# Attention and mixture of experts on one core: exponentials shifted by a running maximum of past batches

## The chip, the cores and the metric

The kernel runs on one core of a Trainium2 chip. A core has TensorE (matrix products, PE in the profile; its weight loads are PEld), VectorE (DVE), ScalarE (ACT), GpSimd (POOL) and SyncE (SP, which here only issues DMAs). The metric is the device time of one execution in microseconds. Before the change it is 1301.42 us, the median of 3 runs (1299.91 to 1301.48).

## The reference, cut to what matters

```python
# q, k, v: 8 batches x 8 heads x 576 rows x 64, standard normal x 0.1
scores = q @ k.T / sqrt(64)                              # 576 x 576 a head
kth  = 32nd largest of each row
scores = where(scores >= kth, scores, -1e9)
scores = scores - max(scores, axis=-1)
attn = exp(scores); attn = attn / (sum(attn) + 1e-9)     # per row
x = attn @ v                                             # heads side by side: 4608 rows x 512
# then top-1 mixture of 8 experts on x: w_gate 512 x 8, w1 512 x 1024, relu, w2 1024 x 512,
# each row scaled by its gate's softmax value
```

Only the 32 largest scores of a row take part. A softmax doesn't change if another number than the row's own maximum is subtracted, as long as the exponentials and their sum are shifted alike.

## The kernel before, in words

**Stages.** First attention over all batches, then the experts. The attention stage has 144 steps of two row tiles (128 rows x 576 scores each); 9 steps are a group `n` of four heads, 18 steps a batch `b`. The stage is a software pipeline: in pass `t` of the loop at line 996 the program issues, in this order, the exponentials of step t-4 (`exps`), the masks of step t-2 (`softmax`), the scores of step t+3 (`scores`, `scores_left`), the products with v of step t-5 (`av`), the transposes of step t-3 (`transp`), and the selection of step t (`topk`). Each engine takes its own instructions in that order; semaphores order the engines.

**One step.** TensorE writes the scores of two row tiles to PSUM; ScalarE copies them to an SBUF tile `sb` (7 pairs of buffers) and SyncE stores them to DRAM as well (for the search below). VectorE runs 24 MAX8 of 48 scores each (line 1016; the 8 largest of each twelfth of a row). `topk` then merges these lists: its list `two` is issued right behind the 24 MAX8, its list `three_` is kept as `delayed` and issued between the MAX8 of the next step, one item behind every second MAX8 (lines 1014 to 1023). In `two` there are two 72-wide MAX8 (`second`), which write places 1 to 8 of the row's work area `v`, and `minus`, which writes places F0 = 8 to 15 from the tile `mid`. `three_` ends in a GpSimd product that makes `nb`: the row's maximum (times -0.125) and its 32nd value (times just under -1). ScalarE's Sign with `nb` as bias marks which scores are under the 32nd value and counts them (`cnt`); GpSimd adds the marks to `sb` (line 471), so that dropped scores become hugely negative.

**The shift.** Line 468 spreads the row's negated maximum to a 128 x 128 bf16 tile `nr` on GpSimd. `transp` first writes these maxima to the transposed scores' PSUM tile `tt` with four bf16 matmuls against an identity (line 484), then adds nine transposes of the scores to them (line 487). `exps` takes the exponential of all of `tt`. The sum of a row is made apart, in `j_sums`, from the 32 values that VectorE found, shifted by the same `nr`.

**Jobs.** What isn't done in every step (loading and turning q and k, sums, writing rows, searching and redoing the rows whose count isn't 32, routing) are generators in lanes. Each says what it needs next (`need(dve=1.0)`, a PSUM bank, a spot), and `advance` lets each lane take at most one part a pass, in order of due time, while the engines' limits (line 52) allow. Parts are put into queues: `dq` for VectorE (issued one at a time between the items of `two`), `aq` for ScalarE, `gq` for GpSimd (at the end of the pass), `pq` for TensorE ahead of the next scores and `lq` for TensorE behind the transposes. `j_find` looks up to 128 rows of a batch whose count is off; it makes `key`, then an index `fl` on VectorE, and gathers the rows; `j_redo` and `j_patch` compute them again; `j_route` assigns experts.

Of the kernel before, what the change touches and what calls it, by code (L numbers as in the profile page):

```python
# [46 lines left out]
TADV = 5  # L47
FREE = (1, 2, 3, 4, 5)
# [3 lines left out]
LIMITS = dict(pool=3.5, act=1.6, dve=2.6, pe=3.0)  # L52
# [3 lines left out]
def attention_moe(ctx, tc, q, k, v, w_gate, w1, w2, out):  # L56
# [130 lines left out]
    nc.vector.memset(factors[:, :, 0], -0.125)  # L187
# [53 lines left out]
    NBB = []  # L241
    for i in range(2):
        NBB.append(jobs.tile([128, NLT, 2], F32, name=f"nb{i}", bufs=1))
# [8 lines left out]
    VQ, CNT, NB, NR = {}, {}, {}, {}  # L252
# [4 lines left out]
    cell, held, att_open = [1], [0], [True]  # L257
# [13 lines left out]
    def need(**k):  # L271
        return k
# [23 lines left out]
    three = psum.tile([128, NB9 * 128], F32, name="tt")  # L296
# [110 lines left out]
    def topk(t, us):  # L407
# [12 lines left out]
        mid = work.tile([128, 2, 8], F32, name="mid", bufs=1)  # L420
# [13 lines left out]
        def second(i):  # L434
# [12 lines left out]
        two.append((minus, (v[:, :, F0:V0, None], mid[:, :, :, None])))  # L447

# [78 lines left out]
    def j_sums(n):  # L527
# [3 lines left out]
        nr = NR[n].rearrange("p (s i) x -> p i s x", i=2)[:, :, :, 0:1]  # L531
# [10 lines left out]
        yield need(pool=0.5)  # L542
# [1010 lines left out]
```

## Time and profile before

| | |
|---|---|
| median of 3 runs | 1301.42 us (1299.91 to 1301.48) |
| profiled execution | 1295.44 us |
| its span, first to last instruction | 1293.4 us |
| busy in the span: PE, DVE, ACT, POOL | 1230.2, 1016.9, 819.1, 859.2 us |
| PE weight loads (PEld) | 972.3 us |
| mean granted TensorE clock | 0.987 |

The table is from one execution under the hardware profiler. Busy time of an engine is the time in which one of its instructions was recorded; an instruction that waits for a semaphore isn't busy. Two neighbouring records of one engine can overlap, since an engine begins an instruction while the one before still runs out. Matmul ends are modelled. A wait is named by the instruction whose semaphore came last.

### The profile page before, as it was taken

What the parts mean: (1) busy time and instruction counts of PE and PEld (TensorE: products, weight loads), DVE (VectorE), ACT (ScalarE), POOL (GpSimd) and SP (SyncE); (2) the same over time, 40 slices, a digit from 0 to 9 for tenths busy, and PEclk for the clock granted to TensorE, in tenths of its full rate; (3) what the DMA queues carried; (4) which work ended last, traced back from release to release, by engine and by line L of the source; (5) the groups of instructions that cost most, each with busy time, mean ns of one, the idle gap of its engine ahead of it and who ended that gap; (6) DMA issues with size and microseconds to landing.
All of it is one profiled execution on the core that took longest, in us unless ns stands there. A gap on an engine that the chain in (4) does not pass through costs nothing.

```text
span 1293.4 us, 33358 instructions
## 1 busy us (share of the span) xinstructions
PE 1230.2 (95%) x10223; PEld 972.3 (75%) x10223; DVE 1016.9 (79%) x6585; ACT 819.1 (63%) x1675; POOL 859.2 (66%) x1172
## 2 busy tenths in 40 slices
PE   5999999999999999998998988999999999999997
PEld 2677776776776776776675766889899999888996
DVE  6999999999999999999999995846683333433763
ACT  3998898898897897897896863332333233233442
POOL 3777876787886886886886886756554333244654
PEclk8999999999999999999999999999999999999999
DMA  6655664664664664664664444645555334346773
GB/s 175 205 169 179 181 205 140 178 192 143 188 181 134 182 183 139 175 189 140 175 190 130 150 126 130 200 124 165 158 163 171 115 106 119 107 156 221 220 210 101
DMA packets 269788, 210.70 MB, mean 163 GB/s; under 512 B 134854, under 2 KB 212834, under 8 KB 269600
## 3 DMA queue, kind: packets, MB, share of 16 engines
q1 hardware_dynamic: 259216, 185.62, 48.3%
q0 software_dynamic: 9152, 22.58, 5.4%
q8 instruction: 82, 1.34, 0.5%
q14 instruction: 106, 0.87, 0.2%
q10 hardware_dynamic: 1232, 0.30, 0.1%
HBM read 102.29 MB, written 107.40 MB: 162 GB/s over the span
## 4 chain that ended last, share of the span: by engine, by line
PE 56%; DVE 21%; POOL 8%; ACT 5%; issue 4%; DMA 4%; SPq 1%; POOLq 0%; ACTq 0%; DVEq 0%
PE ph L1199 16%; PE y L1214 15%; DVE vq L1016 10%; PE px L501 5%; PE pt L260 5%; PE ps L362 5%; POOL sb L471 5%; PE tt L487 4%; DVE vq L1023 4%; PE tt L484 2%; ACT sb L364 1%; DMA sc<-sb 1%; PE mt L1179 1%; PE px L377 1%; ACT sg L470 1%
## 5 line engine op out<-in xcount | busy, mean ns | idle before, releaser
L471 POOL TENSOR_TENSOR sb<-sb,sg 128x576 f32<-128x576 f32 x288 | 369.2, 1291 | 141.4 <-ACT sg L470 82.9
L1016 DVE MAX8 vq<-sb 128x8 f32<-128x48 f32 x3456 | 420.5, 203 | 3.3 <-ACT sb L364 2.6
L949 POOL TENSOR_TENSOR wl<-r,wh 128x512 fp32r<-128x512 f32 x102 | 132.5, 1301 | 206.6 <-DVE wh L948 201.4
L501 PEld LDWEIGHTS px<-et,rv 128*64 128x64 f32 x3200 | 160.2, 139 | 111.7 <-issue 53.2
L470 ACT ACTIVATE sg<-sb,nb 128x576 int8<-128x576 f32 x288 | 223.5, 776 | 25.7 <-POOL nb L1019 19.9
L501 PE MATMUL px<-et,rv 128*64 128x128 f32 (+1 forms) x3200 | 193.8, 270 | 6.3 <-ACT r_et L260 4.4
L1200 ACT ACTIVATE hh<-ph 128x320 fp32r<-128x320 f32 (+2 forms) x128 | 56.1, 438 | 218.8 <-PE ph L1199 196.9
L362 PE MATMUL ps<-qk 64*128 64x512 f32 (+1 forms) x576 | 182.6, 641 | 3.1 <-ACT sb L364 2.6
L492 ACT ACTIVATE et<-tt 128x1152 f32<-128x1152 f32 x144 | 163.1, 1133 | 30.1 <-PE tt L487 29.9
L364 ACT ACTIVATE sb<-ps 128x1024 f32<-128x1024 f32 x144 | 146.8, 1019 | 49.2 <-PE ps L362 49.1
L487 PE MATMUL tt<-turner,sb 128*128 128x128 f32 x1296 | 167.1, 274 | 1.0 <-POOL sb L471 0.9
L1199 PE MATMUL ph<-xh,wh 128*128 128x320 f32 (+2 forms) x504 | 161.0, 319 | 0.0
L1199 PE MATMUL ph<-xh,wl 128*128 128x320 f32 (+2 forms) x504 | 156.5, 310 | 0.0
L1199 PE MATMUL ph<-xl,wh 128*128 128x320 f32 (+2 forms) x504 | 156.3, 310 | 0.0
L1201 DVE SCALAR_TENSOR_TENSOR hl<-ph,hh 128x320 fp32r<-128x320 f32 (+2 forms) x128 | 62.6, 489 | 118.9 <-ACT hh L1200 103.3
L487 PEld LDWEIGHTS tt<-turner,sb 128*128 128x128 f32 x1296 | 139.8, 141 | 1.6 <-POOL sb L471 1.6
L1214 PE MATMUL y<-wh,hl 128*128 128x512 f32 x316 | 124.2, 393 | 2.4 <-DVE hl L1201 2.3
L1214 PE MATMUL y<-wl,hh 128*128 128x512 f32 x316 | 124.3, 393 | 0.0
L1214 PE MATMUL y<-wh,hh 128*128 128x512 f32 x316 | 124.3, 393 | 0.0
L949 DVE TENSOR_TENSOR wl<-r,wh 128x512 fp32r<-128x512 f32 x102 | 85.2, 836 | 49.3 <-ACT wh L946 37.3
L1023 DVE MAX8 vq<-vq 128x8 f32<-128x48 f32 (+1 forms) x576 | 121.6, 212 | 0.0
L1199 PEld LDWEIGHTS ph<-xh,wh 128*128 128x128 f32 x504 | 95.5, 190 | 4.2 <-issue 2.1
(261 smaller groups left out, 2338.2 us busy)
## 6 DMA issues: line engine op xcount, KB each, us to landing
r<-in_moe_w_dram SPq DMA_DIRECT2D x204, 256.0 KB
sc<-sb SPq DMA_DIRECT2D x128, 288.0 KB
sc<-sb SPq DMA_DIRECT2D x128, 256.0 KB
rv<-in_v_dram SPq DMA_DIRECT2D x32, 256.0 KB
xs<-xm SPq DMA_DIRECT2D x16, 512.0 KB
rq<-in_q_dram SPq DMA_DIRECT2D x60, 128.0 KB
rk<-in_k_dram SPq DMA_DIRECT2D x60, 128.0 KB
sc<-sb SPq DMA_DIRECT2D x32, 144.0 KB
```

The source lines that it names most:

```text
L362: nc.tensor.matmul(MAINS[:, n], qk[:, 0, w], qk[:, 1, 2 * LEFT:], start=True, stop=True)
L364: nc.scalar.activation(bass.AP(EX[-1].tensor, EX[-1].offset, [list(EX[-1].ap[0]), [S + LEFT, 2], [1, M]]), MAINS, AF.Copy)
L470: nc.scalar.activation(upper(SG[i]), SB[u], AF.Sign, bias=nb[:, i, 1:2], accum_out=CNT[b][:, 2 * lt + i:2 * lt + i + 1])
L471: nc.gpsimd.tensor_tensor(SB[u], SB[u], SG[i], op=OP.add)
L487: nc.tensor.matmul(tt[:, c], x[:, c * 128:(c + 1) * 128], ident, start=False, stop=c in (3, 7, 8), is_transpose=True)
L492: nc.scalar.activation(ET[t], three.rearrange("p (c q) -> p c q", c=NB9), AF.Exp, scale=0.125)
L501: yield lambda kb=kb, blk=blk: nc.tensor.matmul(px[h * 64:(h + 1) * 64], block(rv, p % 2, kb if kb < MAIN else MAIN + n, h), et[:, blk, q] ...
L949: (nc.gpsimd if i else nc.vector).tensor_tensor(lo, r, hi, op=OP.subtract)
L1016: one[m][0](*one[m][1])
L1023: f(*a)
L1199: nc.tensor.matmul(ph, a[:, c, :], x[:, c, s], start=(m == 0), stop=(m == len(seq) - 1))
L1214: nc.tensor.matmul(PY[u, t], a[:, s], x, start=(f == 0 and m == 0), stop=(f == FC - 1 and m == 2))
```

## The change

- `transp` is nine plain transposes. The four matmuls of line 484 and the tile `nr` are gone.
- `exps` subtracts a shift that is the same for a whole batch, as the bias of ScalarE's exponential, read from an SBUF tile `shifts`. For batches 0 and 1 it is 0. For later ones it is the largest row maximum of the batches up to two before, made by a new job `j_peak`: VectorE reduces each partition's maxima, TensorE turns them into a row, ScalarE copies it to SBUF (`running`), VectorE reduces that with the maximum so far, TensorE spreads it, ScalarE copies it to `shifts`.
- `j_sums` keeps each row's own maximum, and multiplies the sum by the exponential of the difference to the shift (two more GpSimd instructions ahead of the exponentials, one behind).
- A row whose maximum lies more than 512 raw score units from the shift is masked wholly (the mask's bias is moved by 2^100: a comparison in `two` on GpSimd, a subtraction in `three_`) or marked in `j_find` (two GpSimd instructions), and is redone with the rows of odd count.
- `minus` moves from the end of `two` to the head of `three_`; `mid` gets two buffers.
- `j_find`'s index `fl` is made by ScalarE instead of VectorE, and the matmuls of the short jobs go to the queue behind the transposes. These jobs use a free part of `tt`'s third PSUM bank (`SMALL`) as a spot instead of a whole bank.
- The planner's limit for ScalarE goes from 1.6 to 2.1.

```diff
-LIMITS = dict(pool=3.5, act=1.6, dve=2.6, pe=3.0)
+LIMITS = dict(pool=3.5, act=2.1, dve=2.6, pe=3.0)
...
-    nc.vector.memset(factors[:, :, 0], -0.125)
+    nc.vector.memset(factors[:, :, 0], -1.0)
...
+    shifts = consts.tile([128, B, 4], F32, name="shifts")
+    nc.vector.memset(shifts[:, 0:2, 0:2], 0.0)
+    nc.vector.memset(shifts[:, 0:2, 2:3], FAR)
+    nc.vector.memset(shifts[:, 0:2, 3:4], FAR)
+    running = [consts.tile([1, 129], F32, name=f"running{i}") for i in range(2)]
+    nc.vector.memset(running[0][:, 128:129], -NEG)
+    row = consts.tile([1, 128], F32, name="row")
+    nc.vector.memset(row, 1.0)
...
-    three = psum.tile([128, NB9 * 128], F32, name="tt")
+    tt_banks = psum.tile([128, 3 * 512], F32, name="tt")
+    three, SMALL = tt_banks[:, 0:NB9 * 128], tt_banks[:, NB9 * 128:]
...
-        mid = work.tile([128, 2, 8], F32, name="mid", bufs=1)
+        mid = work.tile([128, 2, 8], F32, name="mid", bufs=2)
...
         least(1)
         second(1)
-        two.append((minus, (v[:, :, F0:V0, None], mid[:, :, :, None])))
...
-        three_ = [(nc.vector.tensor_reduce, (merged, pairs, AX.X, OP.max)),
+        after = NBT[b % 2][:, 2 * lt:2 * lt + 2]
+        three_ = [(minus, (v[:, :, F0:V0, None], mid[:, :, :, None])),
+                  (nc.vector.tensor_reduce, (merged, pairs, AX.X, OP.max)),
                   (nc.vector.tensor_reduce, (v[:, :, T0], ends, AX.XY, OP.min)),
-                  (nc.gpsimd.tensor_tensor, (nb, v[:, :, 0:T0 + 1:T0], factors, OP.mult))]
+                  (nc.gpsimd.tensor_tensor, (nb, v[:, :, 0:T0 + 1:T0], factors, OP.mult)),
+                  (nc.gpsimd.tensor_tensor, (nb[:, :, 1], nb[:, :, 1], after, OP.subtract))]
+        two.append((nc.gpsimd.tensor_scalar, (after, v[:, :, 0], shift(b)[:, 2:3], BIG, OP.is_gt, OP.mult)))
...
-        if i == 0:
-            n, s = divmod(t, NT)
-            if s == 0:
-                NR[n] = jobs.tile([128, 2 * NT, LEFT], BF, name="nr", bufs=2)
-            nc.gpsimd.tensor_scalar(NR[n][:, 2 * s:2 * s + 2, :], nb[:, :, 0:1].to_broadcast([128, 2, LEFT]), 8.0, None,
-                                    op0=OP.mult)
...
-        r = NR[n][:, 2 * s:2 * s + 2, :]
-        for c, l, first_ in ((slice(0, 4), r[:, 0, 0:1].to_broadcast([128, 128]), True),
-                             (slice(5, 8), r[:, 1, 0:1].to_broadcast([128, 128]), True),
-                             (slice(4, 5), r.rearrange("p a x -> p (a x)"), False),
-                             (slice(8, 9), r[:, 1, 0:1].to_broadcast([128, 128]), True)):
-            nc.tensor.matmul(tt[:, c], l, identb[:, None, :].to_broadcast([128, c.stop - c.start, 128]),
-                             start=first_, stop=False)
         for c in range(NB9):
-            nc.tensor.matmul(tt[:, c], x[:, c * 128:(c + 1) * 128], ident, start=False, stop=c in (3, 7, 8),
-                             is_transpose=True)
+            nc.tensor.transpose(tt[:, c], x[:, c * 128:(c + 1) * 128], ident)
...
-        nc.scalar.activation(ET[t], three.rearrange("p (c q) -> p c q", c=NB9), AF.Exp, scale=0.125)
+        nc.scalar.activation(ET[t], three.rearrange("p (c q) -> p c q", c=NB9), AF.Exp,
+                             bias=shift(t // (2 * NT))[:, 0:1], scale=0.125)
...
-        yield need(pool=1.9, act=0.6)
-        pool(nc.gpsimd.tensor_tensor, both, both, nr.to_broadcast([128, 2, NT, 8 + VALS]), op=OP.add)
+        yield need(pool=2.5, act=0.6)
+        w = both[:, :, :, 7:8]
+        pool(nc.gpsimd.tensor_tensor, both, both, nm.to_broadcast([128, 2, NT, 8 + VALS]), op=OP.add)
+        pool(nc.gpsimd.tensor_scalar, w, nm, -1.0, shift(b)[:, 1:2], op0=OP.mult, op1=OP.add)
+        pool(nc.gpsimd.tensor_scalar, w, w, -1.25 * FAR, 1.25 * FAR, op0=OP.max, op1=OP.min)
         act(nc.scalar.activation, both, both, AF.Exp, scale=0.125)
...
         pool(nc.gpsimd.tensor_scalar, sums, sums, 1e-9, None, op0=OP.add)
+        pool(nc.gpsimd.tensor_tensor, sums, sums, w, op=OP.mult)
...
+    def j_peak(b):
+        nm = NBB[b % 2][:, :, 0]
+        pk = jobs.tile([128, 1], F32, name="r_pk", bufs=1)
+        yield need(dve=0.1)
+        vec(nc.vector.tensor_reduce, pk, nm, axis=AX.X, op=OP.min)
+        yield need(slack=1)
+        yield need(spot=1, pe=0.1)
+        pt, leave = spot("peak")
+        pe_late(nc.tensor.transpose, pt[0:1, 0:128], pk, ident)
+        act(nc.scalar.activation, running[b % 2][:, 0:128], pt[0:1, 0:128], AF.Copy)
+        act(leave)
+        yield need(slack=1)
+        yield need(dve=0.2)
+        best = running[(b + 1) % 2][:, 128:129]
+        vec(nc.vector.tensor_reduce, best, running[b % 2], axis=AX.X, op=OP.min)
+        yield need(slack=1)
+        yield need(spot=1, pe=0.1, act=0.2, pool=0.3)
+        pt, leave = spot("peak")
+        pe_late(nc.tensor.matmul, pt[:, 0:1], row, best, start=True, stop=True)
+        act(nc.scalar.activation, shifts[:, b + 2, 0:1], pt[:, 0:1], AF.Copy, scale=0.125)
+        act(nc.scalar.activation, shifts[:, b + 2, 1:2], pt[:, 0:1], AF.Copy)
+        act(leave)
+        yield need(slack=1)
+        yield need(pool=0.3)
+        pool(nc.gpsimd.tensor_scalar, shifts[:, b + 2, 2:3], shifts[:, b + 2, 1:2], -1.0, FAR, op0=OP.mult, op1=OP.add)
+        pool(nc.gpsimd.tensor_scalar, shifts[:, b + 2, 3:4], shifts[:, b + 2, 1:2], FAR, None, op0=OP.add)
...
+        lw = sm("r_lw", [128, NLT])
+        pool(nc.gpsimd.tensor_scalar, lw, NBB[b % 2][:, :, 0], shift(b)[:, 3:4], BIG, op0=OP.is_gt, op1=OP.mult)
+        pool(nc.gpsimd.tensor_tensor, lw, CNT[b], lw, op=OP.add)
...
-        vec(nc.vector.scalar_tensor_tensor, key, CNT[b], float(2 * TOPK - S), idx1, op0=OP.not_equal, op1=OP.mult)
+        vec(nc.vector.scalar_tensor_tensor, key, lw, float(2 * TOPK - S), idx1, op0=OP.not_equal, op1=OP.mult)
...
-            pe(nc.tensor.matmul, pl[:, 0:2], oh[:, j], rhs[:, j], start=(j == 0), stop=(j == 7))
+            pe_late(nc.tensor.matmul, pl[:, 0:2], oh[:, j], rhs[:, j], start=(j == 0), stop=(j == 7))
         li = sm("r_li", [128, 2])
+        fl = sm("r_fl", [128, 1], I32)
         act(nc.scalar.activation, li, pl[:, 0:2], AF.Copy)
+        act(nc.scalar.activation, fl, li[:, 1:2], AF.Identity, bias=li[:, 0:1], scale=float(NLT + 1))
         act(leave)
         yield need(slack=1)
-        yield need(dve=0.1)
-        fl = sm("r_fl", [128, 1], I32)
-        vec(nc.vector.scalar_tensor_tensor, fl, li[:, 1:2], float(NLT + 1), li[:, 0:1], op0=OP.mult, op1=OP.add)
...
-        pe(nc.tensor.matmul, rk, before, hist[:, :, KB + 1:].rearrange("p e c -> p c e"), start=True, stop=False)
-        pe(nc.tensor.matmul, rk, ones, cum[:, :, 0:KB].rearrange("p e c -> p c e"), start=False, stop=True)
+        pe_late(nc.tensor.matmul, rk, before, hist[:, :, KB + 1:].rearrange("p e c -> p c e"), start=True, stop=False)
+        pe_late(nc.tensor.matmul, rk, ones, cum[:, :, 0:KB].rearrange("p e c -> p c e"), start=False, stop=True)
...
-        for m in range(max(len(one), 5)):
+        for m in range(max(len(one), 9)):
...
+        if m > 2 * NT and m % (2 * NT) == PEAK and m // (2 * NT) + 1 < B:
+            start("peak", j_peak(m // (2 * NT) - 1), t - 9)
```

## Rows read from the trace of the kernel before

**Rows 1.** Stretches: length; busy us (and instructions) of PE, PEld, DVE, ACT, POOL; clock

```profile
12.00:770.00 758.00, 717.82 (x7159) 518.15 (x7156) 743.38 (x6037) 635.25 (x1304) 588.01 (x789) 0.99 0.57 170
900.00:1000.00 100.00, 100.00 (x537) 90.35 (x536) 63.85 (x148) 33.66 (x65) 55.10 (x67) 1.00 0.57 169
```

**Rows 2.** VectorE's waits up to 770 us: sum, times, longest

```profile
DVE turner L984 <- DMA wg<-in_moe_w_gate_dram: 6.1, 1, 6.1
...
DVE r_key L260 <- ACT sg L470: 2.4, 1, 2.4
DVE less L260 <- ACT vq L260: 2.0, 1, 2.0
```

**Rows 3.** Groups up to 441.06 us: count, busy us, mean ns, idle

```profile
L1016 DVE MAX8 vq<-sb 128x8 f32<-128x48 f32 x2016 | 245.1, 204 | 2.7 <-ACT sb L364 2.6
...
L384 ACT ACTIVATE sb<-px 128x128 f32<-128x128 f32 x86 | 23.2, 270 | 2.6 <-PE px L377 2.6
```

**Rows 4.** VectorE's timeline at a step's end: start us, length us, instruction

```profile
440.50 0.23 DVE L1023 MAX8 vq<-vq 128x8 f32<-128x72 f32 x1
440.64 0.17 DVE L1023 MAX8 mid<-low 128x8 f32<-128x24 f32 x1
440.73 0.22 DVE L1023 MAX8 vq<-vq 128x8 f32<-128x72 f32 x1
440.98 0.17 DVE L423 TENSOR_REDUCE vq<-mid 128x16 f32<-128x16 f32 x1
441.07 0.21 DVE L1016 MAX8 vq<-sb 128x8 f32<-128x48 f32 x1
441.19 0.19 DVE L1019 TENSOR_REDUCE vq<-vq 128x16 f32<-128x32 f32 x1
```

**Rows 5.** VectorE's groups by form, 12 to 770 us: count, busy us, mean ns

```profile
L423 DVE TENSOR_REDUCE vq<-mid 128x16 f32<-128x16 f32 x144 | 24.6, 171 | 4.9
...
L260 DVE TENSOR_TENSOR hist<-oh,valid 128x40 bf16<-128x40 f32 x5 | 6.3, 1255 | 0.0
L260 DVE COPY hist<-cum 128x8 bf16<-128x8 bf16 x5 | 6.2, 1248 | 0.0
L260 DVE TENSOR_TENSOR oh<-oh,fm 128x40 f32<-128x40 f32 x6 | 6.1, 1019 | 0.0
...
L260 DVE SCALAR_TENSOR_TENSOR r_fl<-r_li 128x1 int32<-128x1 f32 x7 | 4.9, 696 | 0.0
...
L260 DVE TENSOR_REDUCE less<-vq 128x18 f32<-128x126 f32 x15 | 4.1, 270 | 2.0 <-ACT vq L260 2.0
...
L260 DVE TENSOR_REDUCE fm<-oh 128x5 f32<-128x40 f32 x6 | 1.0, 172 | 0.0
```

**Rows 6.** GpSimd's groups by form, 12 to 770 us

```profile
L471 POOL TENSOR_TENSOR sb<-sb,sg 128x576 f32<-128x576 f32 x286 | 366.7, 1291 | 138.9 <-ACT sg L470 80.4 <-DMA xs<-xm 23.2 <-DMA rv<-in_v_dram 16.6
L468 POOL TENSOR_SCALAR nr<-nb 128x128 bf16<-128x128 f32 x143 | 78.1, 546 | 11.6
L1019 POOL TENSOR_TENSOR nb<-vq,factors 128x4 f32<-128x4 f32 x144 | 29.8, 207 | 5.0 <-DVE vq L1019 5.0
...
L260 POOL TENSOR_SCALAR sums<-sums 128x18 f32<-128x18 f32 x15 | 4.3, 284 | 1.3
```

**Rows 7.** TensorE's timeline, one step's four bf16 matmuls

```profile
448.94 0.67 PE L484 MATMUL tt<-identb,nr 128*128 128x512 bf16 x4
```

**Rows 8.** TensorE's waits, 12 to 770 us

```profile
PE pt L260 <- DVE vq L1023: 6.3, 4, 1.6
```

**Rows 9.** A short stretch; the third number from the end is the granted clock

```profile
489.00:492.60 3.60, 3.60 (x31) 2.82 (x28) 3.60 (x35) 3.01 (x8) 1.83 (x3) 0.53 0.27 87
```

**Rows 10.** The chain of waits behind the last step: start us, length us

```profile
773.30 2.52 POOL sb L471 x2
775.82 1.61 POOL vq L260
...
777.45 0.92 ACT vq L260
```

More of the change, by code (lines that the diff above doesn't have):

```diff
@@ L20 @@
 BIG = 2.0 ** 100
+FAR = 512.0
 NEG = -3.0e38
@@ L47 @@
 TADV = 5
+PEAK = 5
 FREE = (1, 2, 3, 4, 5)
@@ L239, in block, with shift @@
         return rv[:, g, o * D:(o + 1) * D]
-    NBB = []
+    shifts = consts.tile([128, B, 4], F32, name="shifts")
[6 more added lines that the diff above has]
+    nc.vector.memset(row, 1.0)
+    SHIFTED = set(range(2))
+    def shift(b):
+        assert b in SHIFTED
+        return shifts[:, b]
+    NBB, NBT = [], []
     for i in range(2):
+        NBT.append(jobs.tile([128, NLT], F32, name=f"nbt{i}", bufs=1))
         NBB.append(jobs.tile([128, NLT, 2], F32, name=f"nb{i}", bufs=1))
@@ L251, in attention_moe @@
     VV, SB, EX, ET, XT, SCD = {}, {}, [], {}, {}, {}
-    VQ, CNT, NB, NR = {}, {}, {}, {}
+    VQ, CNT, NB = {}, {}, {}
     READY = set()
     pq, aq, dq, gq, lq = [], [], [], [], []
-    cell, held, att_open = [1], [0], [True]
+    cell, small, held, att_open = [1], [1], [0], [True]
     def later(queue):
@@ L303, in spot @@
     def spot(name):
-        if not att_open[0] or name != "left":
+        if not att_open[0]:
             pt = bank()
@@ L307, in spot @@
         held[0] += 1
+        place, count = (NOOK, cell) if name == "left" else (SMALL, small)
         def leave():
             held[0] -= 1
-            cell[0] += 1
-        return NOOK, leave
+            count[0] += 1
+        return place, leave
     def j_prep(p):
@@ L530, in j_sums @@
         both, d, f = d[:, :, :, F0:V0 + VALS], d[:, :, :, V0:V0 + VALS], d[:, :, :, F0:F0 + EXTRA]
-        nr = NR[n].rearrange("p (s i) x -> p i s x", i=2)[:, :, :, 0:1]
+        b = n // 2
+        nm = NBB[b % 2][:, (n % 2) * 2 * NT:(n % 2 + 1) * 2 * NT, 0:1].rearrange("p (s i) x -> p i s x", i=2)
         sums = jobs.tile([128, 2, NT, 1], F32, name="sums")
         less = jobs.tile([128, 2, NT, 1], F32, name="less")
-        yield need(pool=1.9, act=0.6)
-        pool(nc.gpsimd.tensor_tensor, both, both, nr.to_broadcast([128, 2, NT, 8 + VALS]), op=OP.add)
+        yield need(pool=2.5, act=0.6)
[3 more added lines that the diff above has]
+        pool(nc.gpsimd.tensor_scalar, w, w, -1.25 * FAR, 1.25 * FAR, op0=OP.max, op1=OP.min)
         act(nc.scalar.activation, both, both, AF.Exp, scale=0.125)
@@ L541, in j_sums @@
         yield need(slack=1)
-        yield need(pool=0.5)
+        yield need(pool=0.8)
         pool(nc.gpsimd.tensor_tensor, sums, sums, less, op=OP.subtract)
         pool(nc.gpsimd.tensor_scalar, sums, sums, 1e-9, None, op0=OP.add)
+        pool(nc.gpsimd.tensor_tensor, sums, sums, w, op=OP.mult)
         yield need(dve=0.2)
@@ L626, in apart @@
             tc.declare_no_dep(st.ins, o.ins, reason=why)
+    def j_peak(b):
[24 more added lines that the diff above has]
+        pool(nc.gpsimd.tensor_scalar, shifts[:, b + 2, 3:4], shifts[:, b + 2, 1:2], FAR, None, op0=OP.add)
+        yield
+        SHIFTED.add(b + 2)
     def j_find(b):
         sm = lambda name, shape, dt=F32: jobs.tile(shape, dt, name=name, bufs=1)
+        yield need(pool=0.6)
+        lw = sm("r_lw", [128, NLT])
+        pool(nc.gpsimd.tensor_scalar, lw, NBB[b % 2][:, :, 0], shift(b)[:, 3:4], BIG, op0=OP.is_gt, op1=OP.mult)
+        pool(nc.gpsimd.tensor_tensor, lw, CNT[b], lw, op=OP.add)
         yield need(dve=0.3)
         key = sm("r_key", [128, NLT])
-        vec(nc.vector.scalar_tensor_tensor, key, CNT[b], float(2 * TOPK - S), idx1, op0=OP.not_equal, op1=OP.mult)
+        vec(nc.vector.scalar_tensor_tensor, key, lw, float(2 * TOPK - S), idx1, op0=OP.not_equal, op1=OP.mult)
         vec(nc.vector.max, rhs[:, :, 0], key)
@@ L872, in attention_moe @@
     ROUTED = set()
-    lanes = {k: [] for k in ("prep0", "prep1", "sums", "rows", "redo", "patch", "find", "route")}
+    lanes = {k: [] for k in ("prep0", "prep1", "sums", "rows", "redo", "patch", "peak", "find", "route")}
     wants = {}
@@ L887, in advance @@
                 continue
-            want["bank"] = want.get("bank", 0) + want.pop("spot", 0)
             if not att_open[0]:
-                want["bank"] += want.pop("nook", 0)
-            if want.get("bank", 0) > len(free) or want.get("nook", 0) > cell[0]:
+                want["bank"] = want.get("bank", 0) + want.pop("spot", 0) + want.pop("nook", 0)
+            if want.get("bank", 0) > len(free) or want.get("nook", 0) > cell[0] or want.get("spot", 0) > small[0]:
                 continue
@@ L897, in advance @@
             cell[0] -= want.get("nook", 0)
+            small[0] -= want.get("spot", 0)
             wants[name] = next(lane[0][1], lanes)
```

1 line of the change is left out of this document (removed).

## The prediction

> **What bounds the kernel now.** I read the busy times by stretch first. The attention part runs from about 12 to 770 us, and the mixture-of-experts part follows. In attention VectorE is busy 743.4 of 758.0 us, TensorE 717.8, ScalarE 635.3 and GpSimd 588.0; in a stretch of the second part TensorE is busy for all of 100 us and VectorE for 64 [rows 1]. So two engines look full in attention, and the next view says which of them sets the pace. VectorE's waits up to 770 us are few: 6.1 us for the gate weights ahead of the first step, and in the steps themselves 2.4 us (once) and 2.0 us (once) lead the list [rows 2]. Nobody starves it. The counts up to 441.06 us say the same: ScalarE has copied out the last part of 86 score pairs while VectorE has run 2016 of its 48-wide MAX8, 24 to a step, so 84 steps; two whole pairs lie ready [rows 3]. TensorE is close behind, but VectorE is the bound of attention: a microsecond taken from VectorE comes off the end, one taken from TensorE there does not. The second part is TensorE's and the edit doesn't touch it.
>
> The profiled execution took 1295.44 us, 2.04 above its span, and the median of the other runs is 1301.42, 5.98 above it. I sum against 1295.44 and add 5.98.
>
> **Part by part.**
>
> *The moved `minus`.* The timeline of one step's end shows two 72-wide MAX8. Behind the first (440.50) the next, independent instruction starts after 0.14 us, although the first one's record lasts 0.23. Behind the second (440.73) comes `minus`, and it starts after 0.25 us, 0.03 after the MAX8 ended [rows 4]. In the code the two touch the same element: the MAX8 writes places 1 to 8 of the row, `minus` writes from place F0 = 8 on. So I read 0.25 - 0.14 = 0.11 us of stall in every step. In the new order the next step's first 48-wide MAX8 stands between them: it starts 0.14 behind, and `minus` can start 0.12 later (the pitch from 441.07 to 441.19 [rows 4]), 0.26 behind the writer, when the stall is over. Its later reader, `merged`, gets two MAX8 between instead of one, so no new stall there. There are 144 such `minus` [rows 5]; the last has no next step behind it: 143 x 0.11 = 15.7 us. Ends: 0, if the wait returns in another place, and 16.
>
> [...]
>
> *`fl` to ScalarE.* VectorE loses one instruction a batch, seven of them in the stage: 4.9 us, 696 ns each, although it works on one element [rows 5]. Its record overlaps its neighbours by some 0.08 us, so 7 x (0.70 - 0.08) = 4.3 us. Ends: 7 x 0.09 = 0.6 (if the length is a delay that passes to the next instruction) and 4.9. ScalarE does it in a spare moment: it idles 758.0 - 635.3 = 122.7 us in the stage [rows 1].
>
> *The running maximum.* Six batches add two one-input reductions each on VectorE, one over 36 elements, one over 129. Nearest rows: 172 ns (`fm`, 40 elements) and 270 ns (`less`, 126) [rows 5]; less 0.08 of overlap, 6 x (0.09 + 0.19) = 1.7 us. Ends: 1 and 3.2. The five new fills at the start fall into the 6.1 us for which VectorE waits there [rows 2]; without that cover they would cost under 0.5.
>
> *The waits of jobs.* `key` of the search waits 2.4 us once for ScalarE's sums [rows 2]. The search now begins with two GpSimd instructions and asks VectorE a step (758.0 / 144 = 5.26 us [rows 1]) later, so that wait goes: 2.4. What is late next is GpSimd's own part, issued a whole step before. The sums job gets two GpSimd instructions ahead of ScalarE's exponentials, about 2 x 0.28 us by the `sums` row [rows 6]; its 2.0 us wait may stay or grow by 0.6. I count 0 for it.
>
> *TensorE.* Four bf16 matmuls a step go, 0.67 us with some overlap [rows 7], say 0.6. That is worth nothing directly, since VectorE is the bound; it lets scores run further ahead. Were TensorE the bound, 144 x 0.6 = 86 us would show; VectorE's few waits [rows 2] exclude that. The `rank` matmul, which made TensorE wait 6.3 us for VectorE in four places [rows 8], goes behind the transposes.
>
> *GpSimd.* Per step the spread of `nr` (546 ns) goes and two instructions on two elements come; the nearest row is `nb`, 207 ns [rows 6], so -0.13 us; nine steps share three new small ones of some 0.28, so +0.09. Nothing net, in an engine with 170 us idle [rows 1]. But the order matters: the new comparison waits for VectorE's row maximum of the same step, which lies behind its 24 MAX8 (24 x 0.12 = 2.9 us), and GpSimd takes instructions in order. Queued behind it are the step's jobs, the two 1.29 us additions of the step before [rows 6] and their `nb`; ScalarE's signs and TensorE's transposes wait for those. As two score pairs lie ready, I cost it at nothing; the rival below has its price.
>
> *Delays between VectorE and GpSimd.* VectorE's short two-input and bf16 instructions are long beside one-input ones of the same width: `oh` 1019, `hist` 1255 and 1248 ns against `fm` 172 [rows 5]. Those 16 take 18.6 us; at 172 ns they would take 2.8, so 15.9 are delay, which I ascribe to GpSimd's additions. With GpSimd's phase moved, the ends are -16 and, at 1.29 + 0.17 us each, +5. I take 0, the order of its work being nearly the same.
>
> *After the last step* GpSimd's additions, its part of the last sums job and ScalarE's exponentials stand in the chain, 773.30 to 778.37 us [rows 10]. There come 0.6 us for the two new instructions; the four matmuls and the `nr` of the last steps go. Zero, ends -4 and +2.
>
> Sum: -15.7 - 4.3 + 1.7 - 2.4 = -20.7; 1295.4 - 20.7 = 1274.7 profiled, 1280.7 as the median.
>
> **Rivals.**
>
> A. *The move saves nothing:* the stall comes back at the new place, or is a drain that any order pays. Then -4.3 + 1.7 - 2.4 = -5.0: 1296.4. For it: only 0.01 us of margin in the new spacing. Against it: in the old order the same kind of neighbour ran without a stall. Chance 0.05.
>
> B. *Another engine becomes the bound, half-way:* VectorE waits now and then, and half the gain is left: 1291. For it: in attention TensorE, ScalarE and GpSimd are 95%, 84% and 78% busy. Against it: TensorE, the fullest of the three, loses 0.6 us a step. Chance 0.12.
>
> C. *Slower: GpSimd's queue sets the step.* A step has two additions, 2.58, three small instructions, 0.62, and jobs. Jobs are the 588.0 us less 366.7, 78.1 and 29.8: 113.4 us, 0.79 a step [rows 1, 6]; with the sums job's new ones, 0.88. That is 4.1 us of a step of 5.26. If the wait for VectorE's maximum, and ScalarE's signs behind it, leave GpSimd idle more than 1.16 us a step, it decides. It idles 170 / 144 = 1.18 now, partly because nothing waits for it. At 1.4 us a step takes 5.50, 0.24 more than now: 144 x 0.24 = +35: 1336. Against it: the two pairs in hand must run out first, and the step's wait for VectorE overlaps with its own jobs. Chance 0.05.
>
> D. *Slower by the clock:* TensorE, less busy, spends more time at the half clock. Behind one of its waits for VectorE [rows 8], from 489 us on, the granted clock was 0.53 for 3.6 us, most of it at the lower level, 1.2 GHz [rows 9]. TensorE's busy time a step falls to about 717.8 / 144 - 0.6 = 4.4; at the lower level throughout it would be near 8.8. To pass VectorE's 5.26 - 20.7 / 144 = 5.12 it must lose 0.7 us a step, a sixth of its work at the lower level; at a third, a step takes 5.87: 144 x 0.61 = +88: 1389. That fall was 3.6 us in a batch of 18 steps, 95 us. The Trainium skill, "TensorE: Matmul & The Clock Gate", section "A second HAM failure mode: psum-queue depth-cycling", has small idle gaps between groups of matmuls make the clock swing; the clock of 0.99 over this stage [rows 1] doesn't show it. Chance 0.02.
>
> E. *More than forecast:* delays behind GpSimd shrink and the end shortens, some -12 more: 1269. Chance 0.16.
>
> The forecast has 0.60, with 1274 to 1287 as its own range. The range for 8 in 10 goes from 1267 to 1293: it takes in B and E, half of the delays' gain, and leaves out A, C and D. A measurement of this kernel tells 0.2%, 2.6 us, from no change. A falls mostly on the faster side (0.04), B wholly: faster 0.60 + 0.16 + 0.12 + 0.04 = 0.92, less 0.03 for small losses that no row shows: 0.89; same 0.04; slower 0.07 from C and D.
>
> **What would show it.** In the trace of the changed kernel: a MAX8 between the last 72-wide MAX8 and `minus`, with pitches of 0.14 and 0.12; steps 0.11 us shorter where no job is done; `fl` on ScalarE at about 0.2 us; TensorE's busy share in attention down to some 86%; VectorE still over 98% busy there. The prediction is wrong if VectorE shows repeated waits for `sb`, if GpSimd's comparison heads the chain of waits, if the granted clock in attention falls well under 0.99, or if the second part's length changes by more than a few microseconds.

## The result, and the profile after

The changed kernel takes 1287.88 us, the median of 4 runs (1283.98 to 1289.86), the kernel before beside it 1301.13 us (1299.91 to 1301.48): ratio 0.9896, 95% interval 0.9871 to 0.9921. That is 13.2 us faster, where 20.7 were forecast. The time lies in the range for 8 in 10 and on the right side, but just outside the forecast's own range (1274 to 1287), and nearer to rival B (1291) than to the forecast (1280.7).

The profiled execution took 1289.86 us, 1.76 above its span of 1288.1. That is only 5.6 us under the one before, because that one was 5.98 us quicker than its median; so the traces show where time went, and the sizes come from timed runs. From the first step's first MAX8 to the last step's last one, 752.3 us became 744.8 (-7.5); from there to the experts' first matmul 28.8 became 29.3, and from that to the last output DMA issued 493.9 became 496.3.

The stretches of the changed kernel, columns as in [rows 1]:

```profile
12.00:770.00 758.00, 673.61 (x6653) 488.28 (x6651) 730.95 (x6058) 650.54 (x1338) 608.71 (x1008) 0.98 0.57 171
900.00:1000.00 100.00, 100.00 (x539) 90.47 (x539) 60.78 (x141) 32.51 (x64) 50.38 (x59) 1.00 0.54 158
```

TensorE lost 44 us of busy time, VectorE 12; ScalarE and GpSimd gained 15 and 21. VectorE is no longer full: from 12 us to the last step it is busy 96.8% of the time (98.1% before). Its waits up to 770 us in the changed kernel, the five longest, to hold against [rows 2], are

```profile
DVE rinv L277 <- POOL sums L277: 10.4, 6, 2.3
DVE turner L1026 <- DMA wg<-in_moe_w_gate_dram: 5.9, 1, 5.9
DVE less L277 <- ACT vq L277: 4.0, 1, 4.0
DVE vq L1058 <- ACT sb L383: 3.9, 2, 3.7
DVE r_key L277 <- POOL r_lw L277: 1.9, 1, 1.9
```

The first is new: once in five of the eight batches the reciprocals stand and wait for GpSimd's sums. GpSimd's timeline ahead of one such wait (start us, length us), and the reciprocal that ends it, with its idle time in brackets:

```profile
367.20 1.07 POOL L812 DMA_INDIRECT xs<-r_xa,r_qi  x1 [0.20 <-issue]
368.30 0.42 POOL L277 TENSOR_SCALAR shifts<-shifts 128x1 f32<-128x1 f32 x2
368.65 0.24 POOL L277 TENSOR_TENSOR sums<-sums,less 128x18 f32<-128x18 f32 x1
368.99 0.29 POOL L277 TENSOR_SCALAR sums<-sums 128x18 f32<-128x18 f32 x1
369.36 0.23 POOL L277 TENSOR_TENSOR sums<-sums,vq 128x18 f32<-128x18 f32 x1
```
```profile
369.63 0.20 DVE L277 RECIPROCAL rinv<-sums 128x8 f32<-128x8 f32 x1 [2.22 <-POOL sums L277]
```

New in this row are the two `shifts` and the last `sums`; GpSimd came to it late, though, as the rows below show. The counts up to the end of step 84 (436.26 us in the changed kernel) show the same from the other side: one whole pair is ready, where [rows 3] had two.

```profile
L1058 DVE MAX8 vq<-sb 128x8 f32<-128x48 f32 x2016 | 252.1, 202 | 4.3 <-ACT sb L383 3.9
```
```profile
L403 ACT ACTIVATE sb<-px 128x128 f32<-128x128 f32 x85 | 22.7, 267 | 0.5 <-PE px L396 0.5
```

The move itself did what was forecast. The changed kernel's timeline at the same place as [rows 4]:

```profile
370.58 0.23 DVE L1065 MAX8 vq<-vq 128x8 f32<-128x72 f32 x1
370.73 0.17 DVE L1065 MAX8 mid<-low 128x8 f32<-128x24 f32 x1
370.81 0.22 DVE L1065 MAX8 vq<-vq 128x8 f32<-128x72 f32 x1
370.94 0.20 DVE L1058 MAX8 vq<-sb 128x8 f32<-128x48 f32 x1
371.06 0.17 DVE L442 TENSOR_REDUCE vq<-mid 128x16 f32<-128x16 f32 x1
371.15 0.32 DVE L1058 MAX8 vq<-sb 128x8 f32<-128x48 f32 x2
```

A MAX8 of the next step stands between, 0.13 us behind the writer, and `minus` follows 0.12 later; a step without jobs fell from 4.29 to 4.16 us. The trace's semaphore records say what the gap of [rows 4] was: `minus` waits for VectorE's own semaphore, which the MAX8 before it updates at 440.96, and starts at 440.98; the independent MAX8 at 440.64 has no such wait. In the changed kernel the update comes at 371.04 and `minus` starts at 371.06: the wait is as long as before, but another MAX8 now runs in it.

Who is behind shows in ScalarE's waits for the threshold `nb`, before and after (sum, times, longest):

```profile
ACT sg L470 <- POOL nb L1019: 19.9, 31, 2.6
```
```profile
ACT sg L485 <- POOL nb L1061: 55.2, 82, 2.9
```

GpSimd's own rows, to hold against [rows 6]: the spread `nr` is gone, and `nb` is followed by a subtraction, on which ScalarE's sign waits, and a comparison, which costs half as much again as either.

```profile
L486 POOL TENSOR_TENSOR sb<-sb,sg 128x576 f32<-128x576 f32 x288 | 368.8, 1291 | 93.7 <-ACT sg L485 86.4 <-DMA xs<-xm 3.4 <-DMA sc<-sb 2.4
L1065 POOL TENSOR_SCALAR nbt<-vq,shifts 128x2 f32<-128x2 f32 x144 | 43.7, 303 | 18.9 <-DVE vq L1065 5.2
L1061 POOL TENSOR_TENSOR nb<-vq,factors 128x4 f32<-128x4 f32 x144 | 30.2, 210 | 1.5 <-DVE vq L1061 1.5
L1061 POOL TENSOR_TENSOR nb<-nb,nbt 128x2 f32<-128x2 f32 x144 | 29.0, 201 | 11.3
```

The chain that ended last, by engine, from the page of the kernel before and of the changed one:

```profile
PE 56%; DVE 21%; POOL 8%; ACT 5%; issue 4%; DMA 4%; SPq 1%; POOLq 0%; ACTq 0%; DVEq 0%
```
```profile
PE 50%; ACT 14%; DVE 12%; POOL 9%; issue 7%; SPq 4%; DMA 4%; POOLq 0%; ACTq 0%; DVEq 0%
```

In this execution VectorE's share was nearly halved and ScalarE's nearly tripled: work of the loop in which GpSimd makes the threshold, ScalarE the signs and GpSimd the additions stands in the chain more often. Such shares move: the page of a run below that is nearly the same kernel (reciprocals one step later) has VectorE at 29% and ScalarE at 8%. And the first of the two lines was there to be read beforehand. In the kernel before, VectorE holds 21% of a span of which attention is 58%, so other engines, TensorE above all, already stood in most of attention's chain.

### The profile page after: what moved, and what is told of

It reads as the page before. It is cut to its first block, busy times and chain, and to the rows that moved or that the text cites. A ratio compares the mean times of both kernels' runs of the same rounds, so it can differ in the third digit from the quotient of the medians.

```text
span 1288.1 us, 32718 instructions
## 1 busy us (share of the span) xinstructions
PE 1183.5 (92%) x9665; PEld 938.1 (73%) x9665; DVE 996.2 (77%) x6594; ACT 830.9 (65%) x1701; POOL 876.2 (68%) x1392
## 3 DMA queue, kind: packets, MB, share of 16 engines
q8 instruction: 78, 1.28, 0.4%
## 4 chain that ended last, share of the span: by engine, by line
PE 50%; ACT 14%; DVE 12%; POOL 9%; issue 7%; SPq 4%; DMA 4%; POOLq 0%; ACTq 0%; DVEq 0%
PE ph L1243 16%; PE y L1258 15%; DVE vq L1058 6%; POOL sb L486 5%; ACT sg L485 5%; PE pt L277 5%; PE px L506 4%; PE ps L381 4%; ACT sb L383 3%; PE tt L492 3%; SPq L122 3%; DVE vq L1065 2%; PE mt L1223 1%; ACT qk L277 1%; ACT et L496 1%
## 5 line engine op out<-in xcount | busy, mean ns | idle before, releaser
L1058 DVE MAX8 vq<-sb 128x8 f32<-128x48 f32 x3456 | 432.8, 202 | 6.1 <-ACT sb L383 3.9
L486 POOL TENSOR_TENSOR sb<-sb,sg 128x576 f32<-128x576 f32 x288 | 368.8, 1291 | 93.7 <-ACT sg L485 86.4
L506 PEld LDWEIGHTS px<-et,rv 128*64 128x64 f32 x3200 | 162.8, 140 | 138.5 <-ACT xt L277 56.1
L506 PE MATMUL px<-et,rv 128*64 128x128 f32 (+1 forms) x3200 | 197.0, 273 | 30.4 <-ACT xt L277 20.7
L492 PE MATMUL tt<-turner,sb 128*128 128x128 f32 x1296 | 177.2, 282 | 3.4 <-POOL sb L486 2.2
L496 ACT ACTIVATE et<-tt,shifts 128x1152 f32<-128x1152 f32 x144 | 176.0, 1222 | 2.2 <-PE tt L492 1.6
L991 DVE TENSOR_TENSOR wl<-r,wh 128x512 fp32r<-128x512 f32 x102 | 89.4, 876 | 52.4 <-ACT wh L988 39.1
```

The lines of the kernel that those rows point to most:

```text
L486: nc.gpsimd.tensor_tensor(SB[u], SB[u], SG[i], op=OP.add)
L492: nc.tensor.transpose(tt[:, c], x[:, c * 128:(c + 1) * 128], ident)
L506: yield lambda kb=kb, blk=blk: nc.tensor.matmul(px[h * 64:(h + 1) * 64], block(rv, p % 2, kb if kb < MAIN else MAIN + n, h), et[:, blk, q] ...
L991: (nc.gpsimd if i else nc.vector).tensor_tensor(lo, r, hi, op=OP.subtract)
L1058: one[m][0](*one[m][1])
```

## Experiments

The kernel before took 1292.56, 1298.93, 1295.47 and 1293.74 us on the chips of the four sets below, so sizes are compared as ratios, or as differences within a set.

**First set: which part brings what.** The unchanged kernel once more, as a measure of what can be told apart.

> The kernel before, unchanged, for a second profile of it and as a measure of noise. Every theory: 1300 to 1302 us, ratio 1.000 within 0.002. If its profiled execution again lies some 6 us under its timed ones, the profile of before flatters it; if it lies near 1300, the first one was a quick execution and the comparison of the two profiles (5.3 us of span) understates the change.

Measured: 0.9997 (0.9986 to 1.0007), 1293.0 us. About 0.1% can be told. Its profiled execution took 1294.35 us, 1.35 above its median. So the 5.98 us by which the first profile lay under its median are most likely that one execution's, and the two profiles understate the change.

The move alone:

```diff
-        mid = work.tile([128, 2, 8], F32, name="mid", bufs=1)
+        mid = work.tile([128, 2, 8], F32, name="mid", bufs=2)
...
-        two.append((minus, (v[:, :, F0:V0, None], mid[:, :, :, None])))
...
+        three_ = [(minus, (v[:, :, F0:V0, None], mid[:, :, :, None])),
...
-        for m in range(max(len(one), 5)):
+        for m in range(max(len(one), 7)):
```

> The kernel before with nothing changed but the place of minus (head of the next step's delayed list, mid in two buffers). Theory 1 (the move is worth its whole stall, and the rest of the change costs): steps 0.12 us shorter, 143 x 0.12 = 17 us, so 1284; under the changed kernel's 1288. Theory 2 (the move is worth half, since without the freed TensorE time another engine holds VectorE back; the rest of the change brings the other half): 1292 to 1295, with waits of VectorE for the scores.

And all but the move, `minus` back in its old place in the changed kernel:

```diff
+        two.append((minus, (v[:, :, F0:V0, None], mid[:, :, :, None])))
...
-        three_ = [(minus, (v[:, :, F0:V0, None], mid[:, :, :, None])),
-                  (nc.vector.tensor_reduce, (merged, pairs, AX.X, OP.max)),
+        three_ = [(nc.vector.tensor_reduce, (merged, pairs, AX.X, OP.max)),
```

> The changed kernel with minus put back to the end of its list; all else of the change stays. Theory 1: 1288 + 17 = 1305, above the kernel before by 4. Theory 2: about 1295, still under it. VectorE's gap of 0.25 us behind the second 72-wide MAX8 is back in both.

Measured: the move alone 0.9930 (0.9917 to 0.9943), 8.9 us; all the rest 0.9975 (0.9961 to 0.9988), 3.7 us. Theory 1 falls, and the two parts nearly add up to the whole. Theory 2 has the sizes nearly right; the waits for scores that it foresaw are only a part of what came. In the traces of this set the move takes 19.1 us off VectorE's record (`minus` and `merged`, end to end, over 143 steps), but the steps get only 9.9 us shorter. Some 4.8 us come back as waits (for scores, `key`, `less`, the reciprocals), some 3 us net as longer short two-input instructions, the rest in small pieces. These rows of the unchanged kernel and of the move alone (VectorE by form, 12 to 770 us) show the two instructions that grew most:

```profile
L260 DVE TENSOR_TENSOR po<-po,oh 128x40 f32<-128x40 f32 x5 | 1.0, 198 | 0.0
L260 DVE SCALAR_TENSOR_TENSOR r_key<-cnt,idx 128x36 f32<-128x36 f32 x7 | 1.7, 243 | 2.4 <-ACT sg L470 2.4
```
```profile
L260 DVE TENSOR_TENSOR po<-po,oh 128x40 f32<-128x40 f32 x6 | 7.3, 1224 | 0.0
L260 DVE SCALAR_TENSOR_TENSOR r_key<-cnt,idx 128x36 f32<-128x36 f32 x8 | 5.7, 708 | 4.9 <-ACT sg L470 4.9
```

The last run of the set asks for the reciprocals one step later in the even groups:

```diff
+        if n % 2 == 0:
+            yield need(slack=1)
         yield need(dve=0.2)
         ri = jobs.tile([128, MAIN, 2, 2], F32, name="rinv")
```

> The changed kernel; the sums job asks VectorE for the reciprocals one step later in every second group of heads (those that show the wait). Theory 1 (VectorE's 2.2 us waits for GpSimd's sums, 10.4 us in all, are on the path): 1288 - 10 = 1278. Theory 3 (GpSimd and ScalarE have fallen behind as a whole, so a wait that is avoided returns at the next place): 1285 to 1288, with waits of VectorE for the scores or for later parts of jobs.

Measured: 0.9929 (0.9916 to 0.9942), no better than the changed kernel (0.9896 above, 0.9912 in the next set). The wait for the sums is gone, and `less` (9.7 us), `key` (4.7) and `skip` (4.7) wait instead. That fits theory 3: the group behind VectorE is late as a whole.

**Second set: which engine holds the group.** The changed kernel itself, beside three others.

> The changed kernel as it is, beside the kernel before on the same chip, so that it stands beside the other runs. Its first timing gave a ratio of 0.9896 (0.9871 to 0.9921). With the move alone at 0.9930 and everything but the move at 0.9975: if the two parts add up, 0.9905; if the waits that they cause are partly the same ones, nearer 0.993.

Measured: 1287.41 us, 0.9912 (0.9898 to 0.9926).

Without the mask's two instructions on GpSimd:

```diff
-                  (nc.gpsimd.tensor_tensor, (nb, v[:, :, 0:T0 + 1:T0], factors, OP.mult)),
-                  (nc.gpsimd.tensor_tensor, (nb[:, :, 1], nb[:, :, 1], after, OP.subtract))]
-        two.append((nc.gpsimd.tensor_scalar, (after, v[:, :, 0], shift(b)[:, 2:3], BIG, OP.is_gt, OP.mult)))
+                  (nc.gpsimd.tensor_tensor, (nb, v[:, :, 0:T0 + 1:T0], factors, OP.mult))]
```

> The changed kernel without GpSimd's comparison and subtraction of every step (leaves out the masking of far rows). Theory G (GpSimd's queue is what VectorE now waits for: its small instructions a step take 0.9 us instead of 0.3 and stand ahead of the sums that the reciprocals need): the 10.8 us of waits for GpSimd's sums go, and with them some of the others, so 8 to 11 us less than the changed kernel, and ScalarE's waits for nb (55 us) fall below 30. Theory S (ScalarE's longer exponential holds the group back): at most 3 us less. If neither: within 2 us of the changed kernel.

Measured: 1273.01 us, 0.9794 (0.9781 to 0.9808), 14.4 us under the changed kernel. Theory G holds: the waits for the sums (7.7 us up to 770 us in the changed kernel's trace of this set) are down to 1.0, and ScalarE's for `nb` from 53.7 to 9.5. VectorE's wait for `less` did not go (10.2 and 9.3). The two profiled executions lie only 7.8 us apart; where the rest went they don't show.

Without the bias of the exponential:

```diff
-        nc.scalar.activation(ET[t], three.rearrange("p (c q) -> p c q", c=NB9), AF.Exp,
-                             bias=shift(t // (2 * NT))[:, 0:1], scale=0.125)
+        nc.scalar.activation(ET[t], three.rearrange("p (c q) -> p c q", c=NB9), AF.Exp, scale=0.125)
```

> The changed kernel with the exponentials of the attention weights without a bias (leaves out the shift in them). In both theories the exponential falls from 1222 to about 1133 ns, if the bias that it reads from SBUF is what made it longer. Theory S (ScalarE, 0.09 us a step busier, holds the group back): 5 to 10 us less than the changed kernel, the waits for sums gone. Theory G (GpSimd does): 0 to 2 us less, and the waits for sums still there.

Measured: 0.9907 (0.9892 to 0.9922), 0.65 us under the changed kernel, which can't be told from none. Theory S falls, although the exponential is shorter by 90 ns, in this run and in the changed kernel (ScalarE by form, 12 to 770 us):

```profile
L496 ACT ACTIVATE et<-tt 128x1152 f32<-128x1152 f32 x143 | 161.9, 1132 | 2.1 <-PE tt L492 2.1
```
```profile
L496 ACT ACTIVATE et<-tt,shifts 128x1152 f32<-128x1152 f32 x142 | 173.6, 1223 | 1.6 <-PE tt L492 1.6
```

Three parts of the change put into the kernel before (the move as above, and):

```diff
-            pe(nc.tensor.matmul, pl[:, 0:2], oh[:, j], rhs[:, j], start=(j == 0), stop=(j == 7))
+            pe_late(nc.tensor.matmul, pl[:, 0:2], oh[:, j], rhs[:, j], start=(j == 0), stop=(j == 7))
...
+        act(nc.scalar.activation, fl, li[:, 1:2], AF.Identity, bias=li[:, 0:1], scale=float(NLT + 1))
...
-        yield need(dve=0.1)
...
-        vec(nc.vector.scalar_tensor_tensor, fl, li[:, 1:2], float(NLT + 1), li[:, 0:1], op0=OP.mult, op1=OP.add)
...
-        pe(nc.tensor.matmul, rk, before, hist[:, :, KB + 1:].rearrange("p e c -> p c e"), start=True, stop=False)
...
+        pe_late(nc.tensor.matmul, rk, before, hist[:, :, KB + 1:].rearrange("p e c -> p c e"), start=True, stop=False)
...
```

> The kernel before with three parts of the change alone: the moved minus, fl on ScalarE, and the matmuls of rank and li behind the transposes; the row maxima stay in TensorE's matmuls. If the running maximum is what takes gain back (its GpSimd work and its longer exponential), this beats the changed kernel: the move alone gave 8.9 us, fl takes 0.9 to 2.7 us more and the matmuls some 2, so 12 to 14 us under the kernel before, ratio 0.990. If the lighter TensorE of the running maximum is what pays, it is 3 us or more above the changed kernel.

Measured: 1314.7 us, 1.0129 (1.011 to 1.0147), slower than before, and outside both expectations. The steps took 745.4 us, the way from the last step to the experts 36.3 (28.8 in the changed kernel's trace of this set), and the experts 510.5 (496.5). VectorE now waits for the search's gather, a wait that the changed kernel doesn't have:

```profile
DVE r_v L260 <- DMA r_sb<-sc,r_at: 9.1, 4, 2.9
```

In the experts TensorE idles 14.1 us instead of 4.9, the longest time for VectorE's `xl` (TensorE's waits from 750 us on):

```profile
PE mt L1178 <- DVE xl L1180: 7.2, 2, 5.8
```

Taken apart, these parts cost. Why VectorE was late for the experts, and what took the rest of their 14 us, was not settled.

**Third set: load or order on GpSimd, and TensorE's share.** The threshold without the link of two instructions, at the price of one more:

```diff
-                  (nc.gpsimd.tensor_tensor, (nb, v[:, :, 0:T0 + 1:T0], factors, OP.mult)),
-                  (nc.gpsimd.tensor_tensor, (nb[:, :, 1], nb[:, :, 1], after, OP.subtract))]
+                  *((nc.gpsimd.tensor_scalar, (nb[:, i, 1:2], v[:, i, T0:T0 + 1], -BELOW, after[:, i:i + 1], OP.mult, OP.subtract))
+                    for i in range(2))]
...
+        two.append((nc.gpsimd.tensor_scalar, (nb[:, :, 0], v[:, :, 0], -1.0, None, OP.mult)))
```

> The changed kernel with the same result, GpSimd's work in another order: two instructions of one column each form the masked threshold straight from VectorE's minimum, and ScalarE's first sign waits for the first of them alone; the negated row maximum is formed behind the comparison. One small instruction a step more in all, one less ahead of ScalarE's sign. Leaving the mask out took 14.4 us off the changed kernel (0.9794 against 0.9912). If GpSimd's link between VectorE's minimum and ScalarE's sign is what it costs (0.28 us a step), half of that comes here: 5 to 8 us less than the changed kernel, ratio about 0.986. If it is the load of GpSimd's queue, 0 to 5 us more than the changed kernel.

Measured: 1316.87 us, 1.0154 (1.0139 to 1.0169). By ratio that is 2.4%, some 31 us, above the changed kernel, far more than the expectation had even for the load. It speaks for the load and against the link, but not cleanly: only the first of the two signs has a shorter link, while the second waits for both instructions. GpSimd's rows of this run by form, 12 to 770 us, and VectorE's wait for it:

```profile
L1062 POOL TENSOR_SCALAR nb<-vq,nbt 128x1 f32<-128x1 f32 x278 | 83.7, 312 | 15.1 <-DVE vq L1062 1.3
L1066 POOL TENSOR_SCALAR nbt<-vq,shifts 128x2 f32<-128x2 f32 x139 | 43.9, 316 | 18.9 <-DVE vq L1066 5.1
L1066 POOL TENSOR_SCALAR nb<-vq 128x2 f32<-128x2 f32 x139 | 33.5, 241 | 11.0
```
```profile
DVE rinv L277 <- POOL sums L277: 23.8, 11, 5.6
```

Only 139 of the 144 steps fall into this stretch now, and the reciprocals wait 11 times. And four bf16 matmuls a step, as those of [rows 7], put back:

```diff
+        for c in (slice(0, 4), slice(5, 8), slice(4, 5), slice(8, 9)):
+            nc.tensor.matmul(tt[:, c], identb, identb[:, None, :].to_broadcast([128, c.stop - c.start, 128]),
+                             start=True, stop=True)
         for c in range(NB9):
             nc.tensor.transpose(tt[:, c], x[:, c * 128:(c + 1) * 128], ident)
```

> The changed kernel with four bf16 matmuls a step of the old shapes ahead of the transposes (their result is overwritten). The prediction cost them at nothing, because VectorE sets the pace: then within 2 us of the changed kernel, ratio 0.990 to 0.993. If TensorE's 0.6 us a step is part of what delays the group behind VectorE, as GpSimd's small instructions are, 5 to 15 us more than the changed kernel: ratio 0.996 or above.

Measured: 0.9947 (0.9932 to 0.9962), against 0.9912 for the changed kernel in another set: some 4.5 us more, between the two expectations. TensorE's relief is worth a little, not nothing; the two ratios stand in different sets, and their intervals lie just apart.

**Fourth set: a lighter threshold.** The same result with one GpSimd instruction less a step:

```diff
-                  (nc.gpsimd.tensor_tensor, (nb, v[:, :, 0:T0 + 1:T0], factors, OP.mult)),
-                  (nc.gpsimd.tensor_tensor, (nb[:, :, 1], nb[:, :, 1], after, OP.subtract))]
-        two.append((nc.gpsimd.tensor_scalar, (after, v[:, :, 0], shift(b)[:, 2:3], BIG, OP.is_gt, OP.mult)))
+                  (nc.gpsimd.tensor_tensor, (nb[:, :, 1], after, v[:, :, T0], OP.subtract))]
+        two.append((nc.gpsimd.tensor_scalar, (after, v[:, :, 0], shift(b)[:, 2:3], -BIG, OP.is_gt, OP.mult)))
...
-        nc.scalar.activation(upper(SG[i]), SB[u], AF.Sign, bias=nb[:, i, 1:2], accum_out=CNT[b][:, 2 * lt + i:2 * lt + i + 1])
+        nc.scalar.activation(upper(SG[i]), SB[u], AF.Sign, bias=nb[:, i, 1:2], scale=1.0 + 2.0 ** -23, accum_out=CNT[b][:, 2 * lt + i:2 * lt + i + 1])
...
+        pool(nc.gpsimd.tensor_scalar, nm, VQ[n][:, :, 0:NT * PITCH].rearrange("p i (s x) -> p i s x", x=PITCH)[:, :, :, 0:1],
+             -1.0, None, op0=OP.mult)
...
```

> The changed kernel with the same result and less work on GpSimd: the masked threshold of a step is one subtraction (the factor just below one goes into the scale of ScalarE's sign), and the negated row maxima are formed once for nine steps. GpSimd's small instructions a step go from three to two, some 0.28 us less; leaving two of the three out took 14.4 us off, and one slower one more cost some 31. If GpSimd's load is what took the gain back, 6 to 12 us less than the changed kernel, ratio 0.982 to 0.987. If only the mask's own two instructions together mattered, no change: 0.990 to 0.992.

Measured: 1274.43 us (1271.83 to 1274.68), 0.9854 (0.984 to 0.9868): faster than both kernels. Its page shows VectorE back in the chain, level with TensorE, and VectorE is busy 715.8 of the 726.0 us from 12 us to the last step (98.6%; before 98.1%, in the changed kernel 96.8%):

```profile
PE 42%; DVE 41%; ACT 5%; POOL 4%; issue 4%; DMA 2%; SPq 1%; POOLq 0%; DVEq 0%; ACTq 0%
```

The busy time of the threshold's and the mask's instructions within the steps is 29, 79, 100 and 167 us without the mask, with this edit, in the changed kernel and with one instruction more; the ratios are 0.9794, 0.9854, 0.9912 and 1.0154.

Last, the move's worth where GpSimd has room: `minus` back (the edit of the first set) without the mask.

> The changed kernel without the mask's two GpSimd instructions a step (leaves out the masking of far rows) and with minus back in its old place, to stand against the run without the mask alone (0.9794). If the move is worth its whole stall (15.7 us) when GpSimd has room, the ratio is 0.9915 or near it; if it is worth about 9 us in any surroundings, as in the kernel before (8.9) and in the changed one, 0.986 to 0.987.

Measured: 1283.28 us, 0.9922 (0.9908 to 0.9936), against 0.9794 with the move. By ratio the move brings 1.28%, 16.6 us, there; by the medians on two chips 10.3, by the two profiled spans (1280.8 and 1274.8) 6.0. The ratio speaks for the full stall, the traces don't, and the two kernels didn't run in one set: how large the worth is stays open. That it is larger than with the mask is beyond the intervals, as far as ratios of different sets compare: there the same pair, without the move (0.9975) and with it (0.9912), lies 0.6% apart. Read the other way, the mask costs 0.5% without the move (0.9975 against 0.9922) and 1.2% with it.

## Why the prediction came out as it did

- **The moved `minus`, -15.7: the mechanism right, the term too large.** The stall, the new spacing and `merged` without a stall came as forecast, 0.13 us a step rather than 0.11. Alone it brought 8.9 us. The text gave the end at 0 "if the wait returns in another place", and then took the other end; the runs show half of it returning. The time stayed in the range for 8 in 10 because that range took in rival B, not because this term held.
- **The sentence that failed is "a microsecond taken from VectorE comes off the end".** It rested on VectorE's few waits [rows 2] and on two pairs in hand [rows 3]. Both say who waits now, not how soon another would. ([rows 2] also leaves out one wait ahead of those that the prediction names, 2.6 us for scores at 31.8 us; it changes little.) The chain of the kernel before, where TensorE holds more than VectorE, was a hint, though no proof: with `minus` back in the changed kernel VectorE holds 40% of the chain, and there too the move brought only half. With the shorter step VectorE caught up with jobs that wait for GpSimd or ScalarE once a batch, and no pile of score pairs helps against that; in the run of the move alone the waits that came back, 4.8 us, are some half of what was lost.
- **GpSimd, "nothing net": nearly right by load, wrong in effect.** Three small instructions (210 + 201 + 303 ns) stand where `nb` and `nr` stood (207 + 546 [rows 6]); with the jobs' new ones GpSimd's record up to the experts grew by 17 us, to 651. But the subtraction now lies between VectorE's minimum and ScalarE's sign, where `nr` did not lie, and GpSimd's 170 us of idle time [rows 1] weren't room: 80.4 us of them are waits for ScalarE's signs [rows 6]. GpSimd is also far behind: from the end of VectorE's minimum (the 32nd value) to the end of the step's last threshold instruction the median is 8.5 us in the kernel before, 10.2 in the changed one, 8.0 without the mask and 12.2 with one instruction more. Leaving the mask out gains 14.4 us. What makes the difference to `nr`, which cost as much time, is not separated: the subtraction's place is argued from the order, and beside a delay of 8 to 12 us its own 0.2 us is small.
- **The rest, -4.3 + 1.7 - 2.4 = -5.0: measured as 3.7 in all.** `fl` on ScalarE takes 294 ns (forecast 200) and 4.3 us left VectorE. The running maximum cost 1.6 (1.7). `key`'s wait did not go: it waits 1.9 us for `r_lw`, and the instruction itself rose from 220 to 915 ns, 4.4 us more in all where -2.4 stood. That the 3.7 hold the mask's price as well is shown by the last run: without mask and move the ratio is 0.9922, some 10 us.
- **Not in the sum:** the reciprocals' waits for GpSimd's sums (+11.4 us on VectorE's record), which now stand behind one more GpSimd instruction and the job of the shift. ScalarE's longer exponential was missed too, and costs nothing that could be told.
- **TensorE:** busy 89% of the steps' time (forecast some 86%); its wait of [rows 8] is gone; putting the matmuls back costs 4.5 us, not 0. **The short instructions** of [rows 5]: `fl` and `key` aside, they came out some 6 us shorter in the changed kernel's trace, within the ends given. **After the last step:** +0.5 us, and the experts 2.4 us longer. Of the signs, "VectorE still over 98% busy" failed (96.8%); repeated waits for `sb` did not come (one of 3.7 us, at 32 us).
- **Rivals.** A falls: the move saves, by itself 8.9 us. B's mechanism and nearly its time came: another engine bounds half-way, and it is GpSimd with ScalarE. It had 0.12, since TensorE was taken for the nearest engine; GpSimd, least busy of the four, was the one. C's mechanism is there, and the run with one instruction more comes near its price of 35 (31 us above the changed kernel, 20 above the kernel before), but in the change it doesn't outweigh the gain. D: the clock stayed at 0.98. E didn't come; without the mask the ratio, 0.9794, would make 1274.6, about half-way to it; whether by E's mechanism no run shows.

A rule that would have caught the exponential: the Trainium skill, "ScalarE: Activation LUTs", section "What ACT_TABLE_LOAD costs", gives some 93 ns for each bias or scale read from memory. The trace agrees: 1223 against 1132 ns.

## What to carry to other kernels

When the busiest engine gets faster, look for the next one not by its busy share alone but by the loops that pass between engines once per step. Here GpSimd, the least busy of the four, held the group: small instructions of 0.2 to 0.3 us each, once a step in such a loop, took back 14.4 us, nearly what the saved stall was forecast to give. Count the small instructions on a queue that two others wait for, and first merge them into fewer or do them once for several steps; an order that shortens one link but adds an instruction cost 2.4%. The worth of a saved stall is found by moving it alone, and it depends on how much room the other engines have.

## What the runs showed of the hardware

On GpSimd, an operation on two columns with a per-partition scalar from SBUF took 303 to 318 ns, one on a single column 312, with constants 241, and a two-tensor one 196 to 210: between one and two columns, the form made the difference and not the width. On ScalarE, a bias from SBUF costs the exponential 90 ns. On VectorE, behind a 72-wide MAX8, an instruction that waits for that MAX8's semaphore starts after 0.25 us and one without a wait after 0.14; one independent MAX8 between fills the wait, with pitches of 0.13 and 0.12 us. That the wait stands there because both write place 8 is read from the code; no run took the overlap away.
